# Attention with a learned position bias, then a two-layer MLP: three small loads as repeating transfers, the first layer's weight bound free to run on ScalarE, and a new instruction order

## The chip, the cores and the metric

The kernel runs on one core of one Trainium2 chip. The metric is the device time of one execution in microseconds (us). It is given as the median of three runs with the lowest and highest beside it. A core has five engines that run their own instruction streams in order and meet at semaphores: TensorE (PE, with its weight load PEld), VectorE (DVE), ScalarE (ACT), GpSimd (POOL) and SyncE (SP), which here only issues DMA transfers.

## The reference

The input is q, k, v of shape (4, 8, 576, 64), the three small tensors w1 (1 x 32), b1 (32) and w2 (32 x 8) of a position bias, and the MLP weights w_in (512 x 2048), w_out (2048 x 512) and alpha (2048). w_in and w_out arrive as 64-bit floats.

```
scores = q k^T / 8
x      = log1p(|i - j|) / log1p(max(i, 1))          # one number for each pair of positions
bias_h = relu(x * w1 + b1) @ w2                      # one 576 x 576 bias for each of 8 heads
attn   = softmax(scores + bias)
y      = (attn @ v), rows (b, s), columns (h, d)     # 2304 x 512
h      = y @ w_in;  g = max(h, 0) + alpha * min(h, 0)
out    = g @ w_out                                   # 2304 x 512
```

## The kernel before

The work has four parts that overlap in time.

First, the bias. Its hidden layer has 32 units, so four query positions fill 128 partitions. The constant table `cst` holds log1p of the distance (`R`), of the position (`PSI`), an identity matrix and masks; it is scaled by w1 and b1 once (lines 421 to 431). Each of 36 bias tiles (16 query positions) makes four hidden tiles `relu(R + PSI)` on ACT (line 478), DVE (line 475) or POOL (line 481), multiplies them on PE with `w2b`, a 128 x 32 block-diagonal copy of w2 (line 496), moves the result out of PSUM on ACT (506) or DVE (507), and writes it to a scratch tensor in HBM, from which attention reads it back.

Second, the MLP weights. For each of eight pairs of 128 hidden units (`weights`, "w 0" to "w 7") the raw 64-bit words of w_in and w_out are loaded by SP (line 661), put together to 32-bit floats by three DVE instructions per half (666 and two of 669), bounded by their absolute maximum (w_in on DVE in line 673, w_out on ACT in line 674), and split into a high and a low half-precision part (lines 687 to 694 on ACT or POOL, line 387 on DVE).

Third, attention. Units of two heads and 256 or 320 query rows: scores on PE (601, 602), the minimum for the softmax on DVE (796), the exponential on ACT (799), normalising on POOL or DVE (819, 820), or on POOL and ACT in half precision (809, 810, 812), a turn through PE (828, 838) or a DMA, then attn @ v on PE (849, 857). Batch 0 is in 32-bit floats, batches 1 to 3 are in split half precision.

Fourth, the MLP. Nine chunks of 256 tokens, eight layer pairs each: 24 matmuls of line 927, then ACT 934, DVE 935, 938, 939 or POOL 940, and 12 matmuls of line 946.

Which instruction comes when is no rule in the code. Every operation is entered once with its candidate engines, and three tables at the top of the file decide the rest: `ISSUE` lists the operations in the order in which they are issued, with the chosen engine behind the point; `SLOT` gives each buffer its place; `IDLE` lists how many idle matmuls (line 994, a product with a zero that nobody reads) go ahead of an operation on PE. [...]

The setup that the change touches stands in lines 405 to 440. w1, b1 and w2 are each needed four times, once for each group of 32 partitions, and are loaded by four transfers each (lines 416 to 418), 12 in all. w2b is cleared first (405), its four diagonal blocks are loaded, and line 428 scales it.

Of the kernel before, what the change touches and what calls it, by code (L numbers as in the profile page):

```python
# [9 lines left out]
F32 = mybir.dt.float32  # L10
F16 = mybir.dt.float16
I32 = mybir.dt.int32
AF = mybir.ActivationFunctionType
# [6 lines left out]
P = 128  # L20
# [123 lines left out]
"""  # L144
IDLE = """
30:23 62:2 118:2 90:1 104:1 111:2 683:2 55:3 97:3 132:1 641:2 676:4 959:1 662:1 139:2 634:2 697:1 160:2 669:4 718:5 725:4 704:1 711:1 739:7 388:1
569:3 549:2 767:1 563:1 353:3 596:3 611:1 800:1 419:1 614:1 806:2 814:8 828:4 796:2
"""


# [895 lines left out]
```

## Time and profile before

| | us |
|---|---|
| median of 3 runs | 712.88 |
| lowest and highest run | 711.52 and 715.66 |
| span of the profiled execution, first to last instruction | 709.5 |
| PE busy | 673.0 (95%), 5732 matmuls |
| DVE busy | 513.7 (72%), 1245 instructions |
| ACT busy | 397.4 (56%), 809 instructions |
| POOL busy | 167.7 (24%), 223 instructions |

The profile gives the profiled execution's span; it lists no time of its own around that. The three timed runs lie 2.0 to 6.2 us above the span, the median 3.4 us. The shares of the whole span hide two stages: until about 160 us PE has pauses and DVE has nearly none, and afterwards PE is busy without a pause.

### The profile page before, as it was taken

The numbers are of one execution on the slowest core, as the hardware profiler recorded it, in microseconds if no ns is written. First come the engines' busy times: TensorE is split into PE (matmuls) and PEld (weight loads), VectorE is DVE, ScalarE is ACT, GpSimd is POOL, SyncE is SP. The second block draws the span as 40 slices with busy tenths as digits, with TensorE's granted clock in tenths as the row PEclk, the third lists the DMA queues.
The fourth block names the chain that finished last, engine by engine and source line by source line (L and its number), as shares of the span: only waits on it lengthen the run. The fifth ranks groups of instructions, "written<-read, shape, count | busy, mean of one in ns | idle before, by whom it ended". The sixth has DMA issues, their size and how long they took to land.

```text
span 709.5 us, 15371 instructions
## 1 busy us (share of the span) xinstructions
PE 673.0 (95%) x5732; PEld 422.9 (60%) x5732; DVE 513.7 (72%) x1245; ACT 397.4 (56%) x809; POOL 167.7 (24%) x223
## 2 busy tenths in 40 slices
PE   7988878879999999999999999999999999999997
PEld 2554434445765666666666666666666666666664
DVE  6799999997898789897878777677666755333222
ACT  3888989676776566564565655644454534221321
POOL 1124253223222132221213130221221221111110
PEclk8999999999999999999999999999999999999999
DMA  9899987855589889999999998999788885100000
GB/s 208 218 296 303 289 296 255 283 183 152 117 199 219 185 175 219 222 215 190 219 198 221 194 202 161 177 211 205 170 188 190 173 142 109 19 30 1 30 1 30
DMA packets 236554, 125.89 MB, mean 177 GB/s; under 512 B 204864, under 2 KB 204864, under 8 KB 236480
## 3 DMA queue, kind: packets, MB, share of 16 engines
q1 hardware_dynamic: 233888, 124.90, 75.8%
q8 instruction: 45, 0.74, 0.5%
q10 hardware_dynamic: 2592, 0.01, 0.2%
q14 instruction: 29, 0.24, 0.1%
HBM read 73.87 MB, written 15.61 MB: 126 GB/s over the span
## 4 chain that ended last, share of the span: by engine, by line
PE 71%; DVE 18%; issue 4%; DMA 3%; ACT 2%; POOL 1%; ACTq 0%; SPq 0%; DVEq 0%; POOLq 0%
PE H L927 25%; PE O L946 24%; PE S L602 6%; PE A L849 6%; DVE five L669 3%; DVE fg L796 3%; PE A L857 2%; PE S L496 2%; PE S L828 2%; PE S L576 2%; PE S L601 1%; DMA at<-a 1%; DVE wout L387 1%; DVE mg L935 1%; DVE fg L507 1%
## 5 line engine op out<-in xcount | busy, mean ns | idle before, releaser
L927 PE MATMUL H<-x,win 128*128 128x256 f16 x1728 | 200.7, 273 | 1.3 <-DVE mg L935 1.2
L946 PE MATMUL O<-wout,mg 128*128 128x512 f16 x864 | 198.7, 379 | 1.6 <-DVE st L796 0.8
L927 PEld LDWEIGHTS <-win 128*128 128x128 f16 x1728 | 166.6, 98 | 34.0 <-issue 7.1
L799 ACT ACTIVATE fg<-fg,st 128x576 f32<-128x576 f32 x144 | 110.7, 769 | 55.4 <-DVE st L796 48.0
L946 PEld LDWEIGHTS <-mg 128*128 128x128 f16 x864 | 82.0, 98 | 95.1 <-issue 6.5
L934 ACT ACTIVATE mg<-H,sm 128x256 f32<-128x256 f32 x144 | 62.3, 469 | 135.4 <-PE H L927 121.0
L935 DVE SCALAR_TENSOR_TENSOR mg<-H,sm,mg 128x256 f32<-128x256 f32 x144 | 64.8, 478 | 101.0 <-ACT mg L934 100.7
L796 DVE CUSTOM_DVE_ANT_0 fg<-S,fg 128x576 f32<-128x576 f32 x127 | 93.8, 750 | 17.3 <-PE S L602 14.9
L812 DVE SCALAR_TENSOR_TENSOR a<-fg,st,a 128x576 f16<-128x576 f32 x108 | 90.0, 834 | 21.0 <-POOL a L809 16.1
L809 POOL TENSOR_SCALAR a<-fg,st 128x576 f16<-128x576 f32 x65 | 54.1, 834 | 177.2 <-DMA at<-a 70.1
L940 POOL TENSOR_TENSOR mg<-mg 128x512 f16<-128x512 f32 x33 | 41.2, 1247 | 157.4 <-ACT mg L938 68.1
L496 PE MATMUL S<-at,w2b 128*32 128x79 f32 (+35 forms) x684 | 50.1, 345 | 8.3 <-ACT fg L506 3.4
L602 PE MATMUL S<-qk 64*128 64x288 f16 (+1 forms) x678 | 53.3, 284 | 0.7 <-DVE qk L583 0.7
L849 PE MATMUL A<-at,five 128*64 128x256 f16 (+3 forms) x720 | 51.5, 288 | 0.0
L496 PEld LDWEIGHTS S<-at,w2b 128*32 128x32 f32 x684 | 25.3, 112 | 36.7 <-issue 9.6
L602 PEld LDWEIGHTS <-qk 64*128 64x128 f16 (+1 forms) x720 | 32.7, 96 | 23.4 <-issue 17.2
L849 PEld LDWEIGHTS <-five 128*64 128x64 f16 (+1 forms) x720 | 36.0, 109 | 14.7 <-issue 11.3
L478 ACT ACTIVATE at<-cst 128x464 f32<-128x464 f32 (+17 forms) x62 | 39.1, 658 | 8.0 <-PE S L496 4.5
L810 ACT ACTIVATE a<-fg,st 128x576 f16<-128x576 f32 x43 | 32.9, 769 | 18.6 <-DMA at<-a 11.3
L481 POOL TENSOR_SCALAR at<-cst,npsi 128x416 f32<-128x416 f32 (+15 forms) x32 | 24.9, 785 | 58.0 <-PE S L496 33.2
L994 PE MATMUL H<-sm 128*128 128x512 f16 x111 | 33.5, 412 | 0.9 <-DVE w2b L405 0.9
L819 POOL TENSOR_SCALAR fg<-fg,st 128x576 f32<-128x576 f32 x29 | 23.2, 808 | 44.6 <-DVE st L804 24.6
(148 smaller groups left out, 796.2 us busy)
## 6 DMA issues: line engine op xcount, KB each, us to landing
fg<-scr SPq DMA_DIRECT2D x64, 576.0 KB, 4.9
scr<-fg SPq DMA_DIRECT2D x36, 295.5 KB, 4.5
x<-in_moe_w_in_dram SPq DMA_DIRECT2D x10, 512.0 KB, 5.4
x<-in_moe_w_out_dram SPq DMA_DIRECT2D x10, 512.0 KB, 5.4
fg<-scr SPq DMA_DIRECT2D x32, 144.0 KB, 4.9
out_dram<-mg SPq DMA_DIRECT2D x18, 256.0 KB, 2.6
five<-in_q_dram SPq DMA_DIRECT2D x32, 128.0 KB, 4.4
five<-in_k_dram SPq DMA_DIRECT2D x32, 128.0 KB, 3.8
```

The lines of the kernel that those rows point to most:

```text
L496: nc.tensor.matmul(ps.t[32 * gl:32 * gl + 32, c:n], lhsT=w2b, rhs=x, start=True, stop=True)
L602: return [(lambda a, dst=dst, zq=zq, zk=zk, i=i: nc.tensor.matmul(dst(a), lhsT=tr16(qt)[at, 0, pr, zq, lo:lo + n], rhs=tr16(qt)[at, 1, pr, ...
L796: V(lambda x=x, sl=sl, st=st, ls=ls: nc.vector.tensor_tensor_reduce(out=in_halves(ls[x]()), in0=halves(sl[x].t), in1=in_halves(ls[x]()), s ...
L799: A(lambda x=x, st=st, ls=ls: nc.scalar.activation(ls[x](), ls[x](), AF.Exp, bias=st.t[:, x:x + 1], scale=-1.0, accum_out=st.t[:, 2 + x:3 ...
L809: pl.op([("POOL", 775, lambda x=x, rec=rec, ls=ls, a16=a16: nc.gpsimd.tensor_scalar(a16.t[:, 0:S], ls[x](), rec(), 1.0, op0=ALU.mult, op1= ...
L812: V(lambda x=x, rec=rec, ls=ls, a16=a16: nc.vector.scalar_tensor_tensor(a16.t[:, 640:640 + S], ls[x](), rec(), a16.t[:, 0:S], op0=ALU.mult ...
L849: nc.tensor.matmul(ps.t[64 * hh:64 * hh + 64, 0:w], lhsT=v5[0:hi, zv, n, 2 * pr + hh, :], rhs=at16(at)[0:hi, 5 * za + n, 320 * hh:320 * hh ...
L927: nc.tensor.matmul(hb.t[:, f, :], lhsT=win[:, fp, zw, kb, P * f:P * f + P], rhs=x[:, zx, kb, :], start=(n == 0), stop=(n == 11))
L934: A(lambda f=f: nc.scalar.activation(gf(f), hb.t[:, f, :], AF.Copy, scale=cu[:, f:f + 1]), 470, ky, [hb, t_sig], [(g, f)])
L935: V(lambda f=f: nc.vector.scalar_tensor_tensor(gf(f), hb.t[:, f, :], cs[:, f:f + 1], gf(f), op0=ALU.mult, op1=ALU.max), 475, ky, [hb, t_si ...
L940: ("POOL", 1210, lambda: nc.gpsimd.tensor_tensor(gv(1), g.t, gv(0), op=ALU.subtract))], ky, [g, (gg, 0)], [(gg, 1)], tag="g1", cont=True)
L946: nc.tensor.matmul(ob.t[:, t, :], lhsT=gg.t[:, zg, f, P * t:P * t + P], rhs=wout[:, fp, zw, f, :], start=(first and f == 0 and (zg, zw) == ...
```

## The change

The three small tensors are loaded by one transfer each, whose source repeats itself four times (a step of zero over a dimension of four). w2 goes as a plain 128 x 8 tile `w2r`; w2b is then made by one DVE instruction that multiplies `w2r`, repeated four times along the row, with w1's bound and with a 0/1 mask `OWN`, four new columns of the constant table. The clearing of w2b goes. The bound of w_in gets ACT as a second candidate, in the form that w_out's bound has already. The three tables are new: they hold another issue order, other engines where there is a choice, other buffer places, and 118 idle matmuls at 40 places where before there were 111 at 39.

The diff, with two of the table's lines:

```diff
--- before.py
+++ after.py
@@ -32,119 +32,118 @@
 ISSUE = """
-3 5.1 0 203 2 8.1 1 207 11.1 17 14.1 12 15.1 6.1 16.1 7.1 204 205 9.1 206 13.1 208 10.1 209 18.1 210 215 219 33 211 19 20 21 22 24 34 23 25 29 26 58
...
+2 4.1 9 10 7 0 5 11 13 23 6 8 15 12 19 16 14 3 114.2 457 111 24 20 112.2 21 197 51.2 113 115 22 50.1 72.2 71.1 49.1 198 193 48 199 25 17 52 53.1 104.2
...
 """
 SLOT = """
...
 """
 IDLE = """
-30:23 62:2 118:2 90:1 104:1 111:2 683:2 55:3 97:3 132:1 641:2 676:4 959:1 662:1 139:2 634:2 697:1 160:2 669:4 718:5 725:4 704:1 711:1 739:7 388:1
-569:3 549:2 767:1 563:1 353:3 596:3 611:1 800:1 419:1 614:1 806:2 814:8 828:4 796:2
+20:11 115:2 52:6 73:2 108:1 35:5 59:3 680:3 94:2 213:2 189:5 45:5 66:1 244:1 631:3 947:2 949:2 652:2 129:1 624:3 687:2 150:2 136:2 708:4 715:2 505:1
+694:3 701:5 511:1 743:1 729:5 376:3 542:3 573:7 761:1 775:1 411:2 796:7 786:2 818:2
 """
@@ -298,7 +297,7 @@
     cH = slots("H", opt.get("H", 1), [P, 2, 256], F32, pp)
     win = sb.tile([P, NFP, 2, 4, 256], F16, name="win")
     wout = sb.tile([P, NFP, 2, 2, DM], F16, name="wout")
-    cstt = sb.tile([P, RW + NG + NBT + P + 16], F32, name="cst")
+    cstt = sb.tile([P, RW + NG + NBT + P + 20], F32, name="cst")
     npsi = sb.tile([P, NG], F32, name="npsi")
     sm = sb.tile([P, 384], F32, name="sm")
     w2b = sb.tile([P, 32], F32, name="w2b")
@@ -397,12 +396,13 @@
     EVI = cstt[:, RW + NG:RW + NG + NBT]
     EYE = cstt[:, RW + NG + NBT:RW + NG + NBT + P]
     MASK = cstt[:, RW + NG + NBT + P:RW + NG + NBT + P + 16]
+    OWN = cstt[:, RW + NG + NBT + P + 16:RW + NG + NBT + P + 20]
     w1c, b1c, al, sgn = cols(1), cols(1), cols(16), cols(16)
+    w2r, t_w2r = cols(H), ["w2r"]
     aw, iaw, sg, tb = cols(1), cols(1), cols(1), cols(1)
     KEY0 = pl.begin("init", -1000.0)
     tW = object(), object(), object()
     t_w1, t_b1, t_w2, t_c, t_al, t_aw, t_iaw, t_sg, t_tb, t_R, t_T, t_nal, t_N = [[i] for i in range(13)]
-    V(lambda: nc.vector.memset(w2b, 0.0), SMALL, KEY0, w=[t_w2])
     warm = cols(2)
     t_gap = [["gap"] for _ in range(2)]
     for a in range(2):
@@ -412,12 +412,12 @@
     t_ones = ["ones"]
     V(lambda: nc.vector.memset(one, 1.0), SMALL, KEY0, w=[t_ones])
     A(lambda: nc.scalar.activation(warm[:, 0:1], one, AF.Exp), 250, KEY0, [t_ones], [["warm"]])
-    for i in range(4):
-        DMA(lambda e, i=i: e.dma_start(out=w1c[32 * i:32 * i + 32, :], in_=w1.rearrange("o k -> k o")), 0, KEY0, w=[(t_w1, i)], act_q=True)
-        DMA(lambda e, i=i: e.dma_start(out=b1c[32 * i:32 * i + 32, :], in_=b1.rearrange("(k o) -> k o", o=1)), 0, KEY0 + 1, w=[(t_b1, i)], act_q=True)
-        DMA(lambda e, i=i: e.dma_start(out=w2b[32 * i:32 * i + 32, 8 * i:8 * i + 8], in_=w2), 0, KEY0 + 2, w=[(t_w2, i)], act_q=True)
-    DMA(lambda e: e.dma_start(out=cstt, in_=cst), P * (RW + NG + NBT + P + 16) * 4, KEY0, w=[t_c])
-    DMA(lambda e: e.dma_start(out=al, in_=alpha.rearrange("(c p) -> p c", p=P)), 0, KEY0 + 500, w=[t_al], act_q=True)
+    four = lambda x, n: bass.AP(x.tensor, x.offset, [[0, 4], [n, HID], [1, n]])
+    DMA(lambda e: e.dma_start(out=w1c, in_=four(w1, 1)), 0, KEY0, w=[t_w1], act_q=True)
+    DMA(lambda e: e.dma_start(out=b1c, in_=four(b1, 1)), 0, KEY0 + 1, w=[t_b1], act_q=True)
+    DMA(lambda e: e.dma_start(out=w2r, in_=four(w2, H)), 0, KEY0 + 2, w=[t_w2r], act_q=True)
+    DMA(lambda e: e.dma_start(out=cstt, in_=cst), P * (RW + NG + NBT + P + 20) * 4, KEY0, w=[t_c])
+    DMA(lambda e: e.dma_start(out=al, in_=alpha.rearrange("(c p) -> p c", p=P)), 8192, KEY0 + 500, w=[t_al], act_q=True)
     V(lambda: nc.vector.tensor_reduce(aw, w1c, AX.X, ALU.max, apply_absolute_value=True), SMALL, KEY0, [t_w1], [t_aw])
     V(lambda: nc.vector.tensor_scalar(aw, aw, 2.0 ** -40, None, op0=ALU.max), SMALL, KEY0, [t_aw], [t_aw])
     V(lambda: nc.vector.reciprocal(iaw, aw), SMALL, KEY0, [t_aw], [t_iaw])
@@ -425,7 +425,8 @@
     V(lambda: nc.vector.tensor_tensor(tb, b1c, iaw, op=ALU.mult), SMALL, KEY0, [t_b1, t_iaw], [t_tb])
     V(lambda: nc.vector.tensor_scalar(R, R, sg, None, op0=ALU.mult), dve2(RW, 1), KEY0, [t_sg, t_c], [t_R])
     V(lambda: nc.vector.tensor_scalar(PSI, PSI, tb, None, op0=ALU.mult), dve2(NG, 1), KEY0, [t_tb, t_c], [t_T])
-    V(lambda: nc.vector.tensor_scalar(w2b, w2b, aw, None, op0=ALU.mult), SMALL, KEY0, [t_aw, t_w2], [t_w2])
+    V(lambda: nc.vector.scalar_tensor_tensor(w2b.rearrange("p (g h) -> p g h", g=4), w2r.rearrange("p (o h) -> p o h", o=1).broadcast_to((P, 4, H)), aw,
+                                             OWN.rearrange("p (g o) -> p g o", o=1).broadcast_to((P, 4, H)), op0=ALU.mult, op1=ALU.mult), SMALL, KEY0, [t_aw, t_w2r, t_c], [t_w2])
     V(lambda: nc.vector.tensor_scalar(sgn, al, 1.0, -2.0, op0=ALU.is_gt, op1=ALU.mult), SMALL, KEY0 + 500, [t_al], [t_nal])
     V(lambda: nc.vector.tensor_scalar(sgn, sgn, 1.0, None, op0=ALU.add), SMALL, KEY0 + 500, [t_nal], [t_nal])
     V(lambda: nc.vector.tensor_scalar(npsi, PSI, -1.0, None, op0=ALU.mult), dve2(NG), KEY0, [t_T], [t_N])
@@ -435,7 +436,7 @@
         for gl in range(4):
             nc.tensor.matmul(bps.t[32 * gl:32 * gl + 32, 0:1], lhsT=w2b, rhs=tb, start=True, stop=True)
 
-    PE(beta_mm, 300, KEY0, [t_w2, t_tb], [bps])
+    PE(beta_mm, 300, KEY0, [t_w2, t_tb, t_ones], [bps])
     V(lambda: nc.vector.tensor_copy(beta, bps.t[:, 0:1]), SMALL, KEY0, [bps], [t_beta])
     V(lambda: nc.vector.tensor_scalar(MASK, MASK, beta, None, op0=ALU.mult), SMALL, KEY0, [t_beta, t_c], [t_beta])
@@ -670,7 +671,9 @@
                             for nm, d, e in (("DVE", 685, nc.vector),)]
                     pl.op(alts, key, [raw], [(x, z)], cont=True)
         m = w_mx[:, 2 * fp:2 * fp + 2]
-        V(lambda: nc.vector.tensor_reduce(m[:, 0:1], a.t[:, 0:1024], AX.X, ALU.max, apply_absolute_value=True), 1205, key, [a], [(tok, 0)])
+        pl.op([("DVE", 1205, lambda: nc.vector.tensor_reduce(m[:, 0:1], a.t[:, 0:1024], AX.X, ALU.max, apply_absolute_value=True)),
+               ("ACT", 1245, lambda: nc.scalar.activation(win[:, fp, 1].rearrange("p a b -> p (a b)"), a.t[:, 0:1024], AF.Abs, accum_out=m[:, 0:1]))],
+              key, [a], [(tok, 0), wreg[fp, 0]], tag="wi")
         A(lambda: nc.scalar.activation(wout[:, fp, 1].rearrange("p a b -> p (a b)"), bb.t[:, 0:1024], AF.Abs, accum_out=m[:, 1:2]),
           1245, key, [bb], [(tok, 1), wreg[fp, 1]])
         ar = allmax(m, 2, key, tok)
@@ -1005,7 +1008,8 @@
     t = psi[4 * np.arange(NG)[None, :] + i[:, None]]
     e = np.float32(1.0) / psi[16 * np.arange(NBT)[None, :] + (np.arange(P) // 8)[:, None]]
     m = (np.arange(16)[None, :] >> i[:, None]) & 1
-    return np.ascontiguousarray(np.concatenate([r, t, e, np.eye(P), m], axis=1).astype(np.float32))
+    own = np.arange(4)[None, :] == i[:, None]
+    return np.ascontiguousarray(np.concatenate([r, t, e, np.eye(P), m, own], axis=1).astype(np.float32))
 
 
 # ---- launch: one core; inputs and outputs as the reference has them ----```

What the tables move is seen in the engines' streams. The first place is the start of DVE's stream. Here `mg`, `x_93` and `x_92` are landing places of raw weights, `a_87` and `a_88` are half-precision buffers that are cleared, and `sm` holds all small columns. Before:

```order
L413 MEMSET sm 128x1
L405 MEMSET w2b 128x32
L409 MEMSET a_88 128x640
L409 MEMSET a_87 128x640
L666 TENSOR_SCALAR win<-mg 128x512
L669 SCALAR_TENSOR_TENSOR win<-mg,win 128x512 x2
L666 TENSOR_SCALAR win<-x_93 128x512
L669 SCALAR_TENSOR_TENSOR win<-x_93,win 128x512 x2
L673 TENSOR_REDUCE sm<-win 128x1
L421 TENSOR_REDUCE sm<-sm 128x1
L422 TENSOR_SCALAR sm<-sm 128x1
```

In the changed kernel, at the same place:

```order
L413 MEMSET sm 128x1
L421 TENSOR_REDUCE sm<-sm 128x1
L422 TENSOR_SCALAR sm<-sm 128x1
L409 MEMSET a_87 128x640
L423 RECIPROCAL sm<-sm 128x1
L425 TENSOR_TENSOR sm<-sm 128x1
L427 TENSOR_SCALAR cst<-cst,sm 128x144
L424 TENSOR_TENSOR sm<-sm 128x1
L432 TENSOR_SCALAR npsi<-cst 128x144
L428 SCALAR_TENSOR_TENSOR w2b<-sm,cst 128x32
L426 TENSOR_SCALAR cst<-cst,sm 128x576
L708 TENSOR_REDUCE sm<-sm 128x1
```

The conversion and the bound of the first w_in, which stood ahead of line 421, now come after the whole setup of the bias; line 708 is the maximum of alpha, whose load moved from ACT to SP.

The second place is the start of SP's stream. Before:

```order
L661 DMA mg<-in_moe_w_in_dram 128x2x512
L661 DMA x_93<-in_moe_w_in_dram 128x2x512
L419 DMA cst<-in_const_dram 128x900
L417 DMA sm<-in_b_dram 32x1
L661 DMA mg<-in_moe_w_out_dram 128x1024
L523 DMA five_74<-in_q_dram 128x4x64
```

In the changed kernel:

```order
L419 DMA cst<-in_const_dram 128x904
L417 DMA sm<-in_b_dram 128x1x1
L524 DMA five_76<-in_q_dram 128x4x64
L418 DMA sm<-in_w_dram 128x1x8
L420 DMA sm<-in_moe_alpha_dram 128x16x1
L524 DMA five_76<-in_q_dram 128x4x64
L662 DMA mg<-in_moe_w_in_dram 128x2x512
L662 DMA x_92<-in_moe_w_in_dram 128x2x512
```

The constant table is the first transfer instead of the third, and the raw weights come seventh and eighth.

The third place is ACT's stream at its first bound of a weight. Before, it is w_out's:

```order
L506 ACTIVATE fg<-S_65,cst 128x591
L674 ACTIVATE wout,sm<-wout 128x1024
L478 ACTIVATE at_85<-cst 128x544
L587 ACTIVATE qk_81<-S_64 128x576
L506 ACTIVATE fg<-O_63,cst 128x591
```

In the changed kernel it is w_in's:

```order
L479 ACTIVATE fg<-cst 128x496
L588 ACTIVATE qk_82<-S_65 128x576
L479 ACTIVATE fg<-cst 128x544
L675 ACTIVATE win,sm<-win 128x1024
L588 ACTIVATE qk_82<-S_64 128x576
L479 ACTIVATE fg<-cst 128x400
```

ACT now has seven such bounds of w_in in its stream and DVE one of eight; hidden tiles and copies out of PSUM for the bias stand behind each of them.

## Rows read from the trace of the kernel before

**Rows 1.** Busy time of each engine by stage; columns: window, length, engines, PEclk, DMA share, GB/s.

```profile
0.00:20.00 20.00, 15.10 (x100) 6.13 (x104) 13.05 (x33) 7.71 (x11) 2.58 (x7) 0.83 0.86 190
20.00:40.00 20.00, 18.91 (x248) 10.76 (x240) 15.86 (x37) 16.44 (x26) 4.71 (x7) 1.00 0.96 249
40.00:160.00 120.00, 100.25 (x976) 53.10 (x976) 116.40 (x262) 98.97 (x173) 43.27 (x57) 1.00 0.84 271
160.00:179.08 19.08, 18.83 (x141) 11.11 (x137) 14.05 (x45) 12.90 (x27) 5.99 (x10) 1.00 0.59 148
179.08:700.00 520.92, 515.34 (x4263) 340.16 (x4261) 352.32 (x867) 260.08 (x573) 111.17 (x143) 1.00 0.75 156
```

**Rows 2.** The chain of waits from 50 to 157 us, by engine and line.

```profile
by line: DVE five L669 16.6%; issue 12.5%; DVE fg L796 10.7%; DVE wout L387 7.3%; DVE five L666 5.2%; DVE win L387 4.7%; DVE win L669 4.3%; DVE wout L669 4.3%; DVE at L475 4.1%; DVE fg L507 4.0%; DVE sm L673 3.6%; DVE sm L392 2.7%; DMA five
```

**Rows 3.** Time line of the start; columns: start, length, engine, line, operation.

```profile
0.73 1.85 ACTq L416 DMA_DIRECT2D sm<-in_w_dram  x4
4.72 0.34 SPq L419 DMA_DIRECT2D cst<-in_const_dram  x1
9.57 0.14 DVE L421 TENSOR_REDUCE sm<-sm 128x1 f32<-128x1 f32 x1
11.46 0.24 DVE L428 TENSOR_SCALAR w2b<-w2b,sm 128x32 f32<-128x32 f32 x1
15.68 0.84 ACT L506 ACTIVATE fg<-S,cst 128x591 f32<-128x591 f32 x1 [1.76 <-PE S L496]
```

**Rows 4.** Chain of waits from 0 to 170 us: start, length, what; the last part of w1.

```profile
1.67 4.58 DMA sm<-in_w_dram
```

**Rows 5.** DMA issues of 0 to 40 us; last column: median us to landing.

```profile
cst<-in_const_dram SPq DMA_DIRECT2D x1, 450.0 KB, 3.3
sm<-in_w_dram ACTq DMA_DIRECT2D x4, 0.1 KB, 4.0
```

**Rows 6.** Groups by shape on DVE: count, busy us, mean ns, idle before.

```profile
L673 DVE TENSOR_REDUCE sm<-win 128x1 f32<-128x1024 f32 x4 | 4.9, 1217 | 0.1
L475 DVE TENSOR_SCALAR at<-cst 128x384 f32<-128x384 f32 x4 | 1.5, 417 | 0.7 <-PE S L496 0.7
L475 DVE TENSOR_SCALAR at<-cst 128x528 f32<-128x528 f32 x3 | 1.4, 487 | 0.0
L507 DVE TENSOR_SCALAR fg<-S,cst 128x591 f32<-128x591 f32 x8 | 7.1, 884 | 0.0
L544 DVE TENSOR_REDUCE sm<-five 128x1 f32<-128x1280 f32 x2 | 3.0, 1483 | 0.0
L718 DVE TENSOR_TENSOR sm<-sm 128x1 f32<-128x1 f32 x5 | 1.4, 279 | 0.1
L820 DVE TENSOR_SCALAR fg<-fg,st 128x576 f32<-128x576 f32 x7 | 3.5, 518 | 0.2
L669 DVE SCALAR_TENSOR_TENSOR five<-x,five 128x512 int32<-128x512 int32 x22 | 16.0, 726 | 0.6
```

**Rows 7.** Groups by shape on ACT, w_out's bound and its read-out.

```profile
L674 ACT ACTIVATE wout<-wout 128x1024 f16<-128x1024 f32 x4 | 4.2, 1044 | 0.0
L674 ACT ACTIVATION_READ_ACCUMULATOR wout<-wout 128x1 f32 x4 | 0.8, 190 | 0.0
```

**Rows 8.** PE around 159 us: start, length, line, count of matmuls.

```profile
157.52 0.77 PE L828 MATMUL S<-cst,fg 128*128 128x128 f32 x5
159.77 1.19 PE L601 MATMUL S<-qk 64*64 64x288 f32 x8
```

**Rows 9.** Lines 481, 475, 669: shortest, median and longest of one, in ns.

```profile
L481 POOL TENSOR_SCALAR at<-cst,npsi x32: 522/700/1845, 11.6 to 116.1; 128x416 f32<-128x416 f32 x4, 128x544 f32<-128x544 f32 x3, 128x336 f32<-128x336 f32 x3, 128x560 f32<-128x560 f32 x2
L475 DVE TENSOR_SCALAR at<-cst x35: 370/440/782, 15.7 to 103.1; 128x384 f32<-128x384 f32 x4, 128x400 f32<-128x400 f32 x3, 128x576 f32<-128x576 f32 x3, 128x528 f32<-128x528 f32 x3
L669 DVE SCALAR_TENSOR_TENSOR five<-x,five x22: 674/691/1096, 88.0 to 158.1; 128x512 int32<-128x512 int32 x22
```

**Rows 10.** One stretch of the start with the granted clock (PEclk).

```profile
11.80:19.00 7.20, 6.59 (x61) 2.84 (x61) 4.16 (x12) 5.04 (x9) 2.21 (x3) 0.54 0.97 195
```

211 rows, old and new, of tables (ISSUE, SLOT) are left out of this document.

## Prediction

> **What bounds the kernel now.** Read the stages first [rows 1]. From 179 us to 700 us PE is busy for 515.3 of 520.9 us, so nothing but its own work can end earlier there. Of the first 179.1 us, up to the first matmul of the MLP (line 927), PE is idle for 26.0, and many of its busy spells are idle matmuls. DVE is idle for 19.7 us (6.95 in the first 20 us, 4.14 in the next 20, 3.6 from 40 to 160, 5.0 in the last 19), ACT for 43.1, POOL for 122. The chain of waits from 50 to 157 us [rows 2] is nearly all DVE: the conversion of the raw weights (L669, L666), the split (L387), the softmax minimum (L796), hidden tiles of the bias (L475) and w_in's bound (L673). So the time has two parts: how long DVE takes to bring the MLP's inputs, and how much PE work is left then. The second kernel's gain or loss is the shift of that moment, plus or minus the PE work moved across it.
>
> **The start.** Before, DVE takes w1 only at 9.57 us, behind the conversion and the bound of the first w_in; w2b is ready at 11.70 and the first bias tile leaves PSUM at 15.68 [rows 3]. w1 had landed at 1.67 + 4.58 = 6.25 us [rows 4]. In the changed kernel one w1 transfer leaves ACT at 0.73 us as its only issue, the constants leave SP at about the same time instead of 4.72, and line 421 is DVE's second instruction. With the 4.0 us that a w1 part took at the median and the constants' 3.3 us [rows 5], w1 is there at 4.7 and the constants at 4.0. From line 421 to the end of 428 before were 2.1 us; with one clearing of a half-precision buffer among them I take 2.8. The new w2b needs w2 and the constants, which land no later. So w2b is ready near 7.5 instead of 11.7: 4.2 us sooner. The other bound is w1 landing as soon as the constants, 0.7 us earlier, so 5 us. Cost of the edits themselves: the DVE multiplication that makes w2b replaces a scaling of equal width, the lost clearing is free, and the longer constant table is hidden in its own transfer. Of the queue: alpha and the small loads now stand on SP ahead of the raw weights, which DVE wants only after three hidden tiles; were that cover gone, the price is the delay of the first conversion, bounded by the 3.3 us of the constants' landing.
>
> DVE does not gain those 4.2 us whole: what it did in that time, converting w_in, is only moved behind. It gains idle time. Of its 6.95 us of idle time before 20 us about 3 lie before the first weights land and nearly 3 before 15.7, where its first hidden tile waits for PE. The changed kernel still waits some 4 us for w1, but has conversions to do afterwards. I take 2 us of the 6.95 and 2 of the 4.14 us as gone, since the latter are hidden tiles waiting for PE (the 0.7 us beside L475 [rows 6] are one of these) and the bias chain runs 4 us further ahead. Bounds: none, and 8 us.
>
> **DVE's work up to the first MLP pair.** I count instructions ahead of the first L935 in both streams. Seven of eight bounds of w_in go: 7 x 1.217 = 8.5 us less. Hidden tiles 36 to 29, with 1,888 columns less: from 417 ns at 384 and 487 at 528 columns the slope is 0.00049 us and the base 0.23, so 7 x 0.23 + 0.92 = 2.5 less. One copy out of PSUM less, 0.9; one 1280-wide maximum less, 1.5 [rows 6]. More: two copies of a transposed q or k (not on DVE before; between the 0.52 of L820 and the 0.88 of L507; they read PSUM as L507 does, so 0.85 each) 1.7; eighteen small column operations for the MLP's factors, brought ahead of this place, at up to 0.279, 5.0; two more normalisations of 0.518, 1.0; one more split and a few clearings, an estimate of 1.0. Sum: -13.4 + 8.7 = -4.7 us, of which the 5.0 are merely early and so save DVE time later.
>
> **The other engines.** ACT takes seven bounds, 7 x (1.044 + 0.190) = 8.6 us [rows 7]; it loses four hidden tiles, two copies of q or k, two of turned attention and one exponential and gains one bias copy, which I estimate at -4 together. Net +4.6 against 43.1 us of idle time: hidden, unless one stands in the wrong place (the last rival). POOL gets ten more hidden tiles, 10 x 0.700 = 7.0 us, with 122 idle. PE has ten fewer turn matmuls and four fewer score matmuls ahead of its first MLP pair: 10/5 x 0.77 + 4/8 x 1.19 = 2.1 us [rows 8] that it must do later. The seven additional idle matmuls go where PE waits anyway.
>
> **POOL beside DVE.** Hidden tiles on POOL took 0.522 to 1.845 us, the same on DVE 0.370 to 0.782, a conversion 0.674 to 1.096 [rows 9]: now and then one waits for the other. But the conversions with the longest of these have a mean of 0.726 [rows 6] beside a median of 0.691: 22 x 0.035 = 0.8 us in all 22. I take 1 us for the ten new tiles.
>
> The Trainium skill (SBUF — State Buffer, section SBUF: two separate sides) says that VectorE and GpSimd share a port pair as an exclusive lock: whoever starts first holds it for its whole instruction. By that rule ten tiles could hold DVE for up to ten times their length, and the sum would lose its whole DVE relief. The long outliers agree with a lock; the near-median means say that it seldom catches DVE. It is the third rival below.
>
> **The sum.** The first MLP pair comes at 179.1 - 4 (idle time) - 4.7 (work) + 1 (POOL) = 171.4 us. PE then has 2.1 us more to do, so the end moves by -7.7 + 2.1 = -5.6. The DMA queues are 0.84 to 0.96 busy from 20 to 160 us [rows 1] and move the same bytes; that takes the edge off, but PE's 5.6 us of pauses after 179 us, which a DVE with less work makes fewer, may give as much back. I set both to zero. The span goes from 709.5 to 703.9; the runs lie 3.4 us above the span at the median, so 712.9 becomes 707.3, rounded to **707.0**. Its own range is 702 to 710.
>
> **Rivals.** (1) Nothing at the end: what DVE saves, the DMA queues or ACT take back, since ACT is 82% and DMA 84 to 96% busy in the same stage. Against it: the chain from 50 to 157 us names hardly any transfer. Only the early start and a little of the work remain, -2 us: 711. (2) All of it: 8 us of idle time and 4.7 of work gone, less 2.1: -10.6, 702; with less of the half-speed stretch from 11.8 to 19 us, where the granted clock had a mean of 0.54, between the two levels of 1.2 and 2.4 GHz, and PE was busy for 6.6 us [rows 10], another 3: 699. For it: the first bias tile no longer follows a PE pause. Against it: the new pauses have idle matmuls at other places, and can lower the clock elsewhere at the same price. (3) POOL's ten tiles hold DVE, +7 instead of +1: 0.4 us later than before, 713. The rule above is its ground, the group means are against it. (4) The other side: ACT's order. Each of the seven bounds waits for its conversion on DVE, while ACT's stream stands. One that comes too early waits for up to one half's conversion, 3 x 0.69 = 2.1 us, and takes 1.23 itself: 3.3 us in which no copy of a bias tile leaves PSUM, so that PE, the scratch writes and the reads that attention waits for stop too. Two of the seven at that price take the 5.6 us back; three give 9.9 - 5.6 = +4.3, four +7.6. From three on it is slower; between three and four lies 718. For it: hidden tiles and copies stand right behind each bound. Against it: w_out's eight bounds sit in the same queue now, and ACT's idle time gives room.
>
> **Chances.** Forecast 0.50, nothing 0.20, all 0.12, POOL 0.06, ACT 0.12. A measurement of this kernel can tell about 0.5%, 3.6 us, from no change: below 709.3 is faster, above 716.4 slower. Of the forecast 0.46 lies below 709.3 and 0.04 above; (2) is faster; (1) and (3) are mostly the same, with 0.03 faster; (4) is slower, but for 0.01. Faster 0.61, same 0.28, slower 0.11. The range goes from 700 to 714: it holds (1), (3), the forecast and most of (2).
>
> **What would show it.** Right: line 421 starts on DVE before 6 us, w2b is ready by 8, the first copy of a bias tile starts near 11; L673's column of DVE shrinks to one instruction, and ACT's new bounds stand without long idle time before them; the first L927 starts near 171 us; from there PE is busy as now. Wrong in the start: line 421 after 7 us, or DVE idle for more than 6 us before 20 us. Wrong in DVE's share: the first L927 at 176 us or later. Rival (3): mean hidden tiles on DVE well over 0.45 us, conversions over 0.75. Rival (4): idle time on ACT ahead of w_in's bound of over 1 us apiece. Rival (1): transfers or ACT where DVE now stands in the chain of 50 to 157 us. The forecast fails as a whole if PE's pauses after the first MLP pair exceed the 5.6 us of before by as much as the start gained.

## The result, and the profile after

| | before | after |
|---|---|---|
| median of 4 runs each, us | 712.45 | 705.06 |
| lowest and highest | 711.52, 715.66 | 702.73, 707.39 |
| ratio, 95% interval | | 0.9889, 0.9859 to 0.9918 |
| span of the profiled execution | 709.5 | 700.9 |

Faster by 7.4 us at the median, where 5.9 were forecast. The profiled execution of after took 702.73 us, 1.8 more than its span and the fastest of its four, so the traces show 8.6 us.

Busy time by stage, after, in the columns of [rows 1]:

```profile
0.00:20.00 20.00, 16.29 (x141) 7.16 (x141) 11.24 (x29) 9.33 (x15) 5.42 (x12) 1.00 0.88 215
20.00:40.00 20.00, 18.00 (x216) 9.02 (x214) 18.14 (x35) 16.34 (x28) 10.05 (x14) 1.00 1.04 273
40.00:160.00 120.00, 108.03 (x1060) 60.07 (x1060) 115.71 (x297) 108.70 (x196) 45.74 (x62) 1.00 0.87 277
160.00:164.36 4.36, 4.36 (x32) 1.94 (x28) 2.31 (x10) 2.53 (x7) 0.00 (x0) 1.00 1.09 268
164.36:691.00 526.64, 516.11 (x4279) 343.11 (x4278) 349.00 (x854) 263.99 (x578) 113.49 (x147) 1.00 0.74 154
```

The first MLP pair starts at 164.4 us instead of 179.1: 14.7 earlier, twice the forecast. DVE's work up to it fell from 159.4 us to 147.4, its idle time from 19.7 to 17.0. Stage by stage DVE idles for 8.8 us up to 20 us (6.95 before), 1.9 from there to 40 us (4.14), 4.3 to 160 us (3.6) and 2.05 in the last stretch (5.0). Behind it PE idles 10.5 us in the stretch shown, 5.6 before. Carried to the ends of the two spans, PE's work from the first pair on rose by 1.2 us (519.9 to 521.1) and its idle time by 4.9 (10.5 to 15.5, the last 10 us included): -14.7 + 1.2 + 4.9 = -8.6, the whole difference.

The start, after, in the columns of [rows 3]:

```profile
0.73 1.14 ACTq L416 DMA_DIRECT2D sm<-in_w_dram  x1
0.73 0.39 SPq L419 DMA_DIRECT2D cst<-in_const_dram  x1
4.49 0.15 DVE L421 TENSOR_REDUCE sm<-sm 128x1 f32<-128x1 f32 x1 [3.63 <-DMA sm<-in_w_dram]
6.85 0.25 DVE L428 SCALAR_TENSOR_TENSOR w2b<-sm,cst 128x32 f32<-128x32 f32 x1
10.17 0.84 ACT L507 ACTIVATE fg<-S,cst 128x591 f32<-128x591 f32 x1 [0.78 <-PE S L497]
```

w2b is ready at 7.1 us, the first bias copy starts 5.5 us sooner. In the stretch of [rows 10] the granted clock is now 1.00, where it was 0.54:

```profile
11.80:19.00 7.20, 6.35 (x82) 3.42 (x83) 5.67 (x12) 4.17 (x7) 1.62 (x3) 1.00 1.19 277
```

The chain of waits from 45 to 160 us, after, against the DVE chain of [rows 2]:

```profile
by line: DMA x<-in_moe_w_out_dram 8.8%; ACT fg L507 7.5%; DVE fg L799 7.4%; ACT at L479 7.1%; issue 6.2%; PE S L497 5.9%; ACT fg L802 5.8%; PE O L497 4.7%; ACT wout L677 4.5%; DVE five L670 4.3%; DVE win L386 3.9%; ACT at L841 2.9%; ACT wou
```

No engine leads it. ACT, 99.0 of 120 us busy from 40 to 160 before, has 108.7 now.

Groups on DVE up to the first pair, after, in the columns of [rows 6] (L674 is the bound, L589 the copies of q and k):

```profile
L670 DVE SCALAR_TENSOR_TENSOR five<-x,five 128x512 int32<-128x512 int32 x20 | 13.6, 693 | 0.1
L670 DVE SCALAR_TENSOR_TENSOR win<-mg,win 128x512 int32<-128x512 int32 x8 | 6.5, 814 | 0.1
L589 DVE TENSOR_SCALAR qk<-O 128x576 f32<-128x576 f32 x2 | 1.6, 777 | 0.0
L674 DVE TENSOR_REDUCE sm<-win 128x1 f32<-128x1024 f32 x1 | 1.2, 1211 | 0.0
```

And ACT's new bounds, with the idle time ahead of them in the last column:

```profile
L675 ACT ACTIVATE win<-five 128x1024 f16<-128x1024 f32 x4 | 4.2, 1059 | 1.8 <-DVE five L670 1.8
L675 ACT ACTIVATE win<-win 128x1024 f16<-128x1024 f32 x3 | 3.1, 1043 | 0.0
```

### The profile page after: what moved, and what is told of

It reads as the page before. It is cut to its first block, busy times and chain, and to the rows that moved or that the text cites. A ratio compares the mean times of both kernels' runs of the same rounds, so it can differ in the third digit from the quotient of the medians.

```text
span 700.9 us, 15311 instructions
## 1 busy us (share of the span) xinstructions
PE 667.7 (95%) x5739; PEld 423.2 (60%) x5739; DVE 498.4 (71%) x1227; ACT 402.7 (57%) x822; POOL 174.7 (25%) x233
## 4 chain that ended last, share of the span: by engine, by line
PE 67%; DVE 10%; ACT 9%; DMA 7%; issue 4%; POOL 1%; ACTq 0%; SPq 0%; DVEq 0%; POOLq 0%
PE H L930 24%; PE O L949 22%; PE S L603 5%; PE A L852 5%; DMA at<-a 4%; DVE fg L799 2%; PE S L497 2%; PE S L577 2%; ACT fg L507 2%; PE O L497 2%; ACT at L479 2%; DVE a L815 2%; DMA x<-in_moe_w_out_dram 1%; ACT fg L802 1%; PE A L860 1%
## 5 line engine op out<-in xcount | busy, mean ns | idle before, releaser
L802 ACT ACTIVATE fg<-fg,st 128x576 f32<-128x576 f32 x144 | 110.5, 768 | 32.3 <-DVE st L799 28.8
L815 DVE SCALAR_TENSOR_TENSOR a<-fg,st,a 128x576 f16<-128x576 f32 x108 | 91.8, 853 | 35.8 <-POOL a L812 17.7
L799 DVE CUSTOM_DVE_ANT_0 fg<-S,fg 128x576 f32<-128x576 f32 x127 | 93.6, 749 | 14.8 <-PE S L603 11.1
L812 POOL TENSOR_SCALAR a<-fg,st 128x576 f16<-128x576 f32 x59 | 47.7, 808 | 179.1 <-DMA at<-a 114.5
L943 POOL TENSOR_TENSOR mg<-mg 128x512 f16<-128x512 f32 x37 | 46.2, 1252 | 120.0 <-DVE mg L941 54.4
L603 PE MATMUL S<-qk 64*128 64x288 f16 (+1 forms) x684 | 55.0, 284 | 5.0 <-DVE qk L584 2.9
L603 PEld LDWEIGHTS <-qk 64*128 64x128 f16 (+1 forms) x720 | 34.2, 96 | 24.7 <-issue 19.1
L813 ACT ACTIVATE a<-fg,st 128x576 f16<-128x576 f32 x49 | 37.6, 770 | 17.3 <-DMA at<-a 15.3
L805 POOL TENSOR_SCALAR st<-st 128x2 f32<-128x2 f32 (+1 forms) x41 | 12.7, 309 | 105.2 <-ACT fg L802 101.4
L497 PE MATMUL S<-at,w2b 128*32 128x79 f32 (+38 forms) x432 | 34.2, 334 | 4.7 <-ACT fg L507 2.0
L482 POOL TENSOR_SCALAR at<-cst,npsi 128x320 f32<-128x320 f32 (+14 forms) x34 | 27.7, 819 | 44.2 <-PE S L497 25.6
L479 ACT ACTIVATE at<-cst 128x528 f32<-128x528 f32 (+16 forms) x51 | 32.6, 665 | 10.4 <-DVE cst L426 4.2
L941 ACT ACTIVATE mg<-mg 128x512 f16<-128x512 f32 x36 | 22.6, 627 | 22.7 <-DVE mg L938 16.6
```

The costliest lines, as they stand in the source:

```text
L479: nc.scalar.activation(hb.t[:, 0:wd], R[:, 0:wd], AF.Relu, bias=PSI[:, g:g + 1], scale=1.0)
L497: nc.tensor.matmul(ps.t[32 * gl:32 * gl + 32, c:n], lhsT=w2b, rhs=x, start=True, stop=True)
L603: return [(lambda a, dst=dst, zq=zq, zk=zk, i=i: nc.tensor.matmul(dst(a), lhsT=tr16(qt)[at, 0, pr, zq, lo:lo + n], rhs=tr16(qt)[at, 1, pr, ...
L799: V(lambda x=x, sl=sl, st=st, ls=ls: nc.vector.tensor_tensor_reduce(out=in_halves(ls[x]()), in0=halves(sl[x].t), in1=in_halves(ls[x]()), s ...
L802: A(lambda x=x, st=st, ls=ls: nc.scalar.activation(ls[x](), ls[x](), AF.Exp, bias=st.t[:, x:x + 1], scale=-1.0, accum_out=st.t[:, 2 + x:3 ...
L812: pl.op([("POOL", 775, lambda x=x, rec=rec, ls=ls, a16=a16: nc.gpsimd.tensor_scalar(a16.t[:, 0:S], ls[x](), rec(), 1.0, op0=ALU.mult, op1= ...
```

## The experiments

The theory: the gain is two edits, the early start and the bounds on ACT, each worth what its trace shows. The rival: the edits are worth nothing by themselves and the order of work makes the gain. The edits below change entries of `ISSUE` and `IDLE`; the code is that of after in all of them, so the three repeating loads are in every run. The kernel before, run beside them, had medians of 711.8 to 712.6 us.

**The bounds back on VectorE.**

```diff
-209.1 242.1 308.1 341.1 374.1 407.1 440.1
+209   242   308   341   374   407   440
```

> The changed kernel with its seven bounds of w_in given back to VectorE, at the same places of the order; all else as in the changed kernel. Theory A (up to the first MLP pair the time is VectorE's work plus its pauses): VectorE gets 7 x 1.22 = 8.5 us more work there, the first pair comes 5 to 8 us later, the median goes from 705 to 710 to 713. Rival B (ScalarE, 19.7 to 19.9 of 20 us busy from 60 to 120 us in the changed kernel, is the bound there now): ScalarE loses 8.6 us of work, the first pair comes no later, 702 to 706.

Measured: 710.4 us (708.2 to 714.3), ratio to before 0.9975 (0.9959 to 0.9992): theory A, the bounds are worth 5.4 us here.

**The old start in the new order.**

```diff
-2 4.1 9 10 7 0 5 11 13 23 6 8 15 12 ...
+2 4.1 0 193 1 197 7 5 194 195 196 198 199 200 9 10 11 13 ...
-20:11
+20:23
```

> The changed kernel with the start as it was: the two loads of the first w_in ahead of the constants on SP, and their conversion ahead of the setup of the bias on VectorE, with 23 idle matmuls at the start instead of 11; the repeating loads, the bounds on ScalarE and the rest of the order stay. Theory A (the early start takes VectorE's pauses away): the first copy of a bias tile comes 4 to 5 us later, the first MLP pair 3 to 5 us later, median 708 to 710. Rival C (the bias has slack; later stages take up a late start): the first pair at the same time, 704 to 706.

Measured: 708.7 us (706.2 to 710.1), ratio 0.9940 (0.9918 to 0.9962): theory A again, the start is worth 3.6 us here. The start taken back is not quite that of before, since the repeating loads stay (see the loads alone).

**Both back: the new order alone.** The two edits above together, with 209 behind 200.

> The changed order with both edits of its table taken back: the first w_in's loads ahead of the constants and its conversion ahead of the bias setup, and all eight bounds of w_in on VectorE. The three repeating loads stay. The single runs cost 3.6 us (old start) and 5.4 us (bounds on VectorE) against 705.1. Theory A, the two add: 705.1 + 3.6 + 5.4 = 714, between 712 and 716, so the order alone brings nothing or costs a little. Theory B, both hide the same wait, so only the larger of the two is lost: 709 to 711, and the order alone is worth 2 us or more. Theory C, two losses meet in one stage and compound: above 717.

Measured: 717.4 us (714.8 to 719.0), ratio 1.0067 (1.0043 to 1.0092): slower than before by 5 us, and by 0.4 us in theory C, with theory A's upper bound of 716 within the spread of the runs. Windows from the start to the first pair, of the three kernels in this order:

```profile
0.00:171.45 171.45, 147.60 (x1441) 78.46 (x1441) 155.16 (x376) 130.49 (x228) 62.01 (x86) 1.00 0.87 257
```

```profile
0.00:170.12 170.12, 150.79 (x1454) 79.68 (x1454) 147.31 (x369) 136.69 (x242) 60.35 (x86) 0.99 0.88 259
```

```profile
0.00:177.53 177.53, 149.68 (x1453) 79.58 (x1454) 155.88 (x376) 130.31 (x228) 60.37 (x86) 0.98 0.84 248
```

Read length minus DVE's busy time. The bounds are 7.8 us of DVE work (155.2 against 147.4) and move the first pair by 7.1; the start is 5.8 us of DVE idle time (22.8 against 17.0) and moves it by 5.8; both move it by 13.2. In this order what DVE saves arrives nearly one to one at the first pair. The medians move by less than the first pair: 5.4 us for the bounds, 3.6 for the start, 12.3 for both.

**The early start in the order of before.**

```diff
-2 4.1 193 1 0 197 7 5.1 6.1 194 195 196 198 199 8.1 200 205 209 23 201 9 10 11 12 14 ...
+2 4.1 9 10 7 0 5 11 13 6 15 12 19 16 14 3 20 21 22 193 1 197 194 195 196 ...
-20:23
+20:11
```

> The kernel before with the three repeating loads and with its setup of the bias moved ahead of the first conversion of w_in, on SP and on VectorE, and 11 idle matmuls at the start instead of 23; bounds on VectorE and the rest of the order as before. Theory A: the first copy of a bias tile 4 to 5 us earlier, the end 3 to 5 us earlier, median 708 to 709.5. Rival C: no change, 711.5 to 713.5.

Measured: 712.9 us, ratio 1.0004 (0.9991 to 1.0016). Its clock fell, though: 0.72 from 4 to 12 us, 0.50 from 12 to 20, with PE busy for 3.4 and 4.5 of these 8 us each. So once more with more idle matmuls:

```diff
-20:11 52:2
+20:18 52:8 458:12
```

> The order of before with the early start, as in the run that gained nothing (712.9), but with 7 more idle matmuls behind the setup, 6 more ahead of the first bias tile and 12 ahead of the first alpha matmul, so that PE stands less between 5 and 17 us, where that run showed a granted clock of 0.50 to 0.72 for 14 us. Theory A, the half clock ate the gain of the early start: the clock stays at 1.0 until 20 us, and the time falls by 2 to 4 us, to 708.5 to 710.5. Theory B, the order of before has no use for an earlier bias tile, since DVE's queue is the limit: the clock is mended and the time stays at 711.5 to 713.5.

Measured: 712.8 us, ratio 1.0011 (0.9995 to 1.0027). The clock is 1.00 up to 20 us, the first bias copy comes at 11.34 us instead of 15.68, and still the first pair comes at 180.9:

```profile
0.00:180.87 180.87, 154.71 (x1466) 82.84 (x1467) 159.45 (x374) 136.28 (x236) 56.75 (x80) 0.99 0.82 244
```

The time is theory B's: the first tile's 4.3 us do not come back as less DVE idle time (21.4 us; 19.7 before). By 40 us DVE had done 28.0 us of work against 28.9 before.

**The bounds on ACT in the order of before**, with its start, and then with the early start too.

```diff
-209   242   308   374   341   407   440
+209.1 242.1 308.1 374.1 341.1 407.1 440.1
```

> The order and the start of before, the three repeating loads, and seven of w_in's eight bounds on ScalarE. Nothing is changed at the start, so the clock there is that of before (0.99 and above). Theory A, the bounds pay in any order as they do in the new one, where they are worth 5.4 us: 706 to 709.5. Theory B, in the order of before ScalarE's stream stands at the bounds and gives back what VectorE saves; the first pair comes no earlier than 178 us and the time is 711.5 to 714.

Measured: 711.9 us, ratio 0.9988 (0.9974 to 1.0002).

> As the kernel before with repeating loads and the early setup, and besides with the same seven bounds of w_in on ScalarE that the changed kernel has there; the rest of the order is that of before. So it holds every edit but the new order. Theory A: VectorE's work and pauses fall by 8.5 + 4 us before the first pair, the end moves as in the changed kernel, 703 to 707. Rival D (the new order is what makes the edits pay; in the old one ScalarE waits at the bounds for the conversions): 708 to 716, with over 1 us of idle time on ScalarE ahead of a bound.

Measured: 713.0 us, ratio 1.0009 (0.9997 to 1.0022), with the clock at 0.81 and 0.50 in the two stretches named above. With the added idle matmuls:

> The order of before with both edits, the early start and seven of w_in's bounds on ScalarE, and with the added idle matmuls that hold the clock until 20 us. Theory A, either edit alone only makes room in front of the other's wait, and together they gain in the order of before as well: 704 to 709. Theory B, the order of before waits in turn for PE, transfers and VectorE, so that what VectorE saves stands as idle time: 711 to 713.5, with the first pair at 178 us or later and VectorE idle for more than 24 us before it.

Measured: 715.4 us, ratio 1.0039 (1.0021 to 1.0057); the idle matmuls did not hold the clock here, it was 0.57 from 12 to 20 us. First the bounds alone, then both: the window to the first pair and ACT at the first bound (L677 here; columns: start, length, then in brackets the idle time and what ended it).

```profile
0.00:179.02 179.02, 152.07 (x1452) 80.70 (x1453) 152.84 (x367) 142.41 (x249) 57.31 (x80) 0.98 0.83 247
10.75 1.06 ACT L677 ACTIVATE win<-win 128x1024 f16<-128x1024 f32 x1 [3.86 <-DVE win L672]
16.75 0.84 ACT L509 ACTIVATE fg<-S,cst 128x591 f32<-128x591 f32 x1 [1.76 <-PE S L499]
```

```profile
0.00:183.98 183.98, 153.85 (x1465) 81.89 (x1466) 153.79 (x367) 142.99 (x250) 58.88 (x80) 0.98 0.80 240
13.91 1.06 ACT L677 ACTIVATE win<-win 128x1024 f16<-128x1024 f32 x1 [10.50 <-DVE win L672]
18.64 0.84 ACT L509 ACTIVATE fg<-S,cst 128x591 f32<-128x591 f32 x1 [1.05 <-PE S L499]
```

With the bounds alone DVE is rid of 6.5 us of work and idles for 26.2 us instead of 19.7: against the kernel before, the first pair stands where it was. Not all of that is the bounds'. With the loads alone (next run) DVE idles for 23.8 us already and the first pair comes at 183.4; against that run the bounds bring it 4.4 us forward and the median down by 1.9. (The two profiled executions took 710.86 and 715.75 us, 1.0 below and 2.0 above their medians, so the 4.4 is rather too large.) ACT's 3.86 us ahead of the bound cost little here, since the hidden tiles behind it then wait another 0.45 us for DVE's setup:

```profile
12.34 1.42 ACT L481 ACTIVATE at<-cst 128x560 f32<-128x560 f32 x2 [0.45 <-DVE cst L429]
```

With both edits DVE idles for 30.2 us, and one place of the loss can be seen. The order of before has the first w_in's bound ahead of the first bias tile. With the early start the constants are scaled by 8.6 us, but ACT stands for 10.5 us at the bound, and the first bias copy starts at 18.64 us instead of 11.34 with the early start alone: the early start is undone.

```profile
14.96 1.40 ACT L481 ACTIVATE at<-cst 128x560 f32<-128x560 f32 x2
```

The new order has that bound at 22.62 us, behind the first tiles, with no wait. No run has the order of before with this one bound behind the first tiles or left on DVE, so how much of the failure of both edits is this one place is not shown.

**The loads alone in the order of before.**

> The kernel before with nothing but the three repeating loads in place of its twelve small ones: order, start and bounds as they were. All theories: within 1 us of before, 711 to 713. A gain of 2 us or more would say that the twelve loads' queue time, and not the order, held the start.

Measured: 713.8 us, ratio 1.0019 (1.0007 to 1.0030): 1.3 us slower, so nothing is gained by fewer loads as such. All theories missed this by a little; in its profile DVE takes w1 at 11.79 us (9.57 before). The loads change what stands beside them. Before, SP's issue of the constants waited for 3.0 us until the first half of w_in had landed and went out at 4.72 us [rows 3]; here it goes out at 1.74, the second half of w_in lands 7.5 us after its issue instead of 4.8, and DVE waits for it. Before, then the loads alone (two rows and the window to the first pair):

```profile
6.53 0.42 DVE L666 TENSOR_SCALAR win<-x 128x512 int32<-128x512 int32 x1
```

```profile
1.74 0.46 SPq L421 DMA_DIRECT2D cst<-in_const_dram  x1
8.74 0.43 DVE L669 TENSOR_SCALAR win<-x 128x512 int32<-128x512 int32 x1 [2.15 <-DMA x<-in_moe_w_in_dram]
0.00:183.39 183.39, 153.99 (x1453) 82.02 (x1454) 159.61 (x374) 136.29 (x235) 56.17 (x80) 0.97 0.80 241
```

Why the issue no longer waits the traces do not show. The same pause of 2.1 to 2.2 us stands in the other runs with the old start: the bounds alone, the old start in the new order, and both back. So the 5.8 us of DVE idle time that the early start is worth in the new order hold some 2 us that the loads cost in the old start.

| order | neither edit | early start | bounds on ACT | both |
|---|---|---|---|---|
| of before | 713.8 | 712.8 | 711.9 | 715.4 |
| new | 717.4 | 710.4 | 708.7 | 705.1 |

Medians in us; all eight have the repeating loads. Both runs of the order of before with the early start are those with added idle matmuls; without these they took 712.9 and 713.0. In both runs with both edits the clock fell at the start. From neither edit, the order of before gains 1.9 us by the bounds; its early start lies within the intervals' overlap, and both together gain nothing. The new order gains 7.0, 8.7 and 12.4, and is slower than the order of before without the edits, by 3.7 us, and faster with both, by 10.3. The order changes as a whole here, with its engine choices, buffer places and idle matmuls; which part of it makes the edits pay no run separates.

**ACT relieved.** Since ACT was busy for 59.2 of the 60 us from 60 to 120 us, five of its scalings went to GpSimd.

```diff
-285   288   290   384   389
+285.1 288.1 290.1 384.1 389.1
```

> The changed kernel with five of the scalings that round w_out's and w_in's high parts, at about 80 to 120 us, on GpSimd instead of ScalarE (4.4 us of ScalarE's time). Theory A, ScalarE, busy for 19.7 to 19.9 of 20 us from 60 to 120 us, sets the moment of the first pair together with VectorE: the first pair comes 1 to 3 us before 164.4 and the time falls to 702 to 704. Theory B, VectorE alone sets it (or GpSimd is too slow at it): 705 to 708.

Measured: 707.0 us (704.4 to 707.5), ratio 0.9918 (0.9894 to 0.9942). The stretch in after, then here:

```profile
60.00:120.00 60.00, 53.44 (x583) 27.26 (x582) 57.86 (x142) 59.22 (x104) 18.87 (x26) 1.00 0.92 309
```

```profile
60.00:120.00 60.00, 52.18 (x580) 26.67 (x574) 58.67 (x137) 55.11 (x96) 25.75 (x30) 1.00 0.91 306
```

ACT has 4.1 us less to do and the first pair comes at 166.5, not earlier. ACT at 99% did not set it alone; theory A falls. DVE's work up to the first pair is 149.5 us here instead of 147.4, with the same 369 instructions and the same 17.0 us of idle time, while GpSimd has 7.2 us more to do. Part of the delay is no effect of the edit that can be named: DVE's first hidden tile starts at 11.21 us instead of 10.24, with the clock lower from 4 to 12 us (last section). The time is not clear of after's.

**The pauses behind the first pair.** Nine pieces of PE work were brought ahead of a piece that waits, like this one at 208 us:

```diff
-1083 2190
+2190 1083
```

> The changed kernel with nine pieces of PE work moved ahead of a piece that stood waiting for VectorE or ScalarE after the first MLP pair (the pauses at 178, 208, 219, 233, 253, 286, 311, 333 and 394 us, 0.51 to 1.19 us each, 7.3 us together of the 10.4 us of pauses there). Theory A, the pauses are the new order's own slips and nothing else is behind them: most of the 7.3 us are gained, 698 to 702. Theory B, what is waited for is late by more than a piece of PE work lasts, or the pieces put back make later ones late: the pauses move, and the time stays at 703.5 to 707. Theory C, the attention chain that is put back sets the end: above 707.

Measured: 712.9 us (710.2 to 715.0), ratio 1.0004 (0.9987 to 1.0020): theory C. Waits of PE from the first pair on, in all, times, longest one; after, then here:

```profile
PE S L603 <- DVE qk L584: 2.9, 5, 1.2
PE S L603 <- DVE st L799: 1.8, 2, 1.0
PE H L930 <- DVE mg L938: 1.5, 3, 0.6
```

```profile
PE H L932 <- DVE mg L940: 5.7, 6, 1.8
PE S L605 <- DVE st L801: 3.3, 4, 1.3
PE S L579 <- DVE st L801: 2.2, 2, 1.2
```

The first pair comes at 165.4, one us later than in after. The named waits behind it sum to 16.4 us against 10.4, and PE's own busy time there rises by 2.6. These waits fit the following reading, which no run tests: the scores that were put back come late to DVE, whose order was not changed with them, and the MLP's gates (mg) behind them on DVE come late to PE.

**Without idle matmuls.** `IDLE` is empty.

> The changed kernel without any of its idle matmuls but the table of work the same. Theory A, the order is what gains and the clock falls only for short: the first 160 us show half clock in a few stretches and the time is 706 to 712. Theory B, the clock held up by the idle matmuls is a condition of the gain: the granted clock of the first 40 us is under 0.8 and the time is 713 or more. Theory C, the idle matmuls only cost PE time: below 704.

Measured: 709.1 us (705.8 to 713.4), ratio 0.9956 (0.9931 to 0.9981): theory A. The first pair comes at 171.8 with 146.6 us of DVE work before it, as in after, and a clock below 1 in two stretches:

```profile
20.00:60.00 40.00, 29.80 (x383) 17.37 (x379) 33.33 (x66) 30.51 (x51) 18.40 (x25) 0.87 0.99 280
140.00:160.00 20.00, 15.56 (x88) 9.98 (x88) 17.36 (x55) 15.68 (x33) 6.86 (x11) 0.83 0.53 164
```

The idle matmuls are worth some 4 us. None of the runs beat the changed kernel.

## Why the prediction was right, and where it was not

Direction and size hold, but three of its terms failed. That their errors cancelled in part, DVE's work 7.3 us better than forecast and PE's pauses 4.9 us worse, is luck.

- *The start*: w2b forecast near 7.5, seen at 7.1; first bias copy near 11, seen at 10.2. DVE's idle time up to the first pair fell by 2.7 us, 4 forecast, and not where all 4 were to come from: in the first 40 us it fell by 0.5 only, and before 20 us it rose to 8.8, which is over the 6 us that the prediction named as a sign of a wrong start. From 40 to 160 us it rose by 0.7, and in the last stretch it fell by 3.0. An early first tile moved the pauses; it did not remove them. That the start's worth belongs to the start was an assumption: in the order of before the same early copy brought nothing that can be told from the loads alone.
- *DVE's work*: this step failed, -4.7 us forecast, -12.0 seen. The lengths of DVE's instructions up to the first pair sum to 171.7 us instead of 179.5, so -7.8. The bounds are -8.5 as forecast and the two copies +1.6. The hidden tiles are -1.8, 2.5 forecast; the 1280-wide maximum, -1.5 forecast, gave nothing, since before too it starts behind the first pair, at 181.1 us; the small column operations (lines 720 to 727), +5.0 forecast, are +2.3; three softmax minima that no longer stand ahead give -2.2, which the sum lacked. The other 4.2 us are in no instruction: they overlap more (last section). The count of instructions, up to the first L935 and not up to the first pair, could not show that.
- *GpSimd beside DVE*: +1 us forecast. All 64 conversions (L670) took 46.1 us instead of 45.2, so +0.9. The rise sits in w_in's conversions at the start (814 ns now, 694 for the same group before), not in those into `five` (693, before 726). A hidden tile on DVE took 501 ns at the mean instead of 454, which goes the way of the prediction's sign for rival (3), well over 450. Tiles of 478 columns instead of 437 explain 20 of the 47 ns at the prediction's slope; the rest, 27 ns for each of 29 tiles, is 0.8 us. So rival (3) has the signs of a small price, far from its 7 us, and conversions and GpSimd's tiles stand close to [rows 9]:

```profile
L670 DVE SCALAR_TENSOR_TENSOR five<-x,five x20: 671/686/803, 86.7 to 146.6; 128x512 int32<-128x512 int32 x20
L482 POOL TENSOR_SCALAR at<-cst,npsi x34: 516/681/1533, 7.6 to 88.4; 128x320 f32<-128x320 f32 x5, 128x336 f32<-128x336 f32 x4, 128x544 f32<-128x544 f32 x3, 128x464 f32<-128x464 f32 x3
```

- *PE behind the first pair*: 2.1 us more work forecast, 1.2 seen. Its pauses were set at no change, and that failed: +4.9. They belong to the new order, and PE was not quite without pauses before: PE's named waits from the first pair on sum to 10.4 us in after and to 10.1 in the new order without either edit, to 5.6 before and to between 5.1 and 6.1 in the variants of the old order. The failing test that I named, pauses grown by as much as the start gained, is met against the 2.7 us of idle time and not met against the first pair's 14.7; the time fell, so the test was no test.
- *Rival (1)* would have been read from transfers and ACT in the chain of waits. They are there, and the time fell: the test was wrong. A chain without a leader means here that DVE is no longer alone, not that nothing is gained.
- *Rival (2)* had the half-speed stretch gone, and it is: 1.00 instead of 0.54. What that gave no run separates; in the order of before, a clock held at 1.00 up to 20 us brought the first pair forward by 0.4 us (181.3 to 180.9).
- *Rival (4)*: in the changed kernel ACT idled 1.8 us before the seven bounds, so it did not happen. Its mechanism is real: with both edits in the order of before ACT stood for 10.5 us at the first bound, ahead of its hidden tiles.
- *From span to median*: 3.4 us were added, a profiled execution takes 1.8 more than its span. The traces show 8.6, the medians 7.4; which of after's four runs is typical is not settled by them.

What stays open: against the loads alone, DVE idles in the old order for 2.4 us more with the bounds on ACT and for 6.4 us more with both edits. The place of the first bound explains a part of the second; the rest is not taken apart.

## What to carry to other kernels

An edit and the order around it can act as one change: time either without the other, and in a tuned order read what saved time turns into, idle time of the same engine or an earlier hand-over. Count idle time and work up to the hand-over separately from pauses behind it, since errors in the two cancel in the total. Count up to the same event in both kernels. When small transfers go, look at what is issued earlier for it and what lands later. Do not mend pauses by swapping pieces on one engine while the others keep their order.

## What the runs showed of the hardware

In the rows below an instruction on DVE that does not need the result before it starts before that one's end. Columns: start and length, after:

```profile
100.80 0.41 DVE L667 TENSOR_SCALAR five<-mg 128x512 int32<-128x512 int32 x1
101.25 0.69 DVE L670 SCALAR_TENSOR_TENSOR five<-mg,five 128x512 int32<-128x512 int32 x1
101.86 0.16 DVE L451 TENSOR_SCALAR sm<-sm 128x2 f32<-128x2 f32 x1
101.93 0.42 DVE L667 TENSOR_SCALAR five<-x 128x512 int32<-128x512 int32 x1
102.39 0.69 DVE L670 SCALAR_TENSOR_TENSOR five<-x,five 128x512 int32<-128x512 int32 x1
```

L670, which reads what L667 wrote, begins 0.04 us after its end; L451, which doesn't, begins 0.08 before L670's end. Taken from the time line up to the first pair, such overlaps between rows number 235 before and 299 after; the new order alone has 305, the order of before with the bounds on ACT 224. The lengths of DVE's instructions sum to more than its busy time by 20.1 us before and 24.3 after, by 24.7 in the new order alone and by 19.3 in the order of before with the bounds on ACT. So the spacing belongs to the order. That something put between a DVE instruction and its reader is what makes the same work shorter fits the rows; no run changed that alone. The Trainium skill (VectorE: DVE Perf Modes, section Two Vector instructions with no wait between them) gives a model in which a held instruction starts only when every earlier VectorE instruction has finished. The rows agree that there are two kinds of start; which rule sorts these instructions no run here tested.

The granted clock in two kernels with the same order at the start differs: from 4 to 12 us its mean was 1.00 in after, where PE was busy for 5.9 of these 8 us, and 0.79, between its two levels, with the scalings on GpSimd, where PE was busy for 5.8. Ahead of that the same 11 idle matmuls took 4.88 us in after and 4.07 there, and PE then stood for 1.36 us in after and for 2.23 there before its next matmul. Why the idle matmuls took less time there the traces do not show.
